# Moving the narrowing of weight pieces on VectorE's and ScalarE's queues in a fused attention, soft-MoE and MLP kernel

## The chip, the cores and the metric

The kernel runs on one core of a Trainium2 chip. The metric is the device time of one execution in microseconds (us); the median of three runs of the kernel before is 685.01 us (684.3 to 691.0).

## The reference

Attention over 4 batches of 12 heads, 448 tokens, 64 dimensions, with normalised q and k, gives a matrix `x` of 1792 tokens by 768. A soft mixture of 8 experts with 4 slots each follows, and then a two-layer MLP with a leaky activation:

```python
logits = x @ phi
d = softmax of logits over tokens;  c = softmax of logits over slots
slot_input = (d.T @ x).reshape(E, 4, 768)
h = np.maximum(slot_input[e] @ w1[e], 0.0)        # per expert e
slot_out[e] = h @ w2[e]
x = c @ slot_out
h = x @ w_in
g = np.maximum(h, 0.0) + alpha * np.minimum(h, 0.0)
out = g @ w_out
```

The inputs are float32, but `w_in` and `w_out` are float64 and reach the kernel as pairs of 32-bit words; "narrowing" a piece of them (128 rows by 768) means making float32 numbers of it with integer operations.

## The kernel before, in words

**Stages.** Attention runs up to about 308 us of the profile. The expert stage follows (315 to 417 us), then a short stage that multiplies the slots' outputs S into `w_in` (L1396 to L1447, to about 428 us), and then the main loop of the MLP (L1528 to L1530), which runs to the end.

**Order.** From attention on, the program's order is written out by hand (`manual_schedule`): each engine works through its own queue in the order in which the program issues instructions, and an instruction that waits holds up all behind it on that engine. All large transfers are issued by SP (SyncE), in program order too.

**The expert loop** (`for e in range(E)`). For each of 8 experts: PE multiplies the slots' inputs by the first layer, 24 matmuls of 512 columns (L1339); ScalarE copies the two halves to `h_sb` (L1350); PE transposes them (L1353); VectorE sums columns (L1355) and takes the maximum with 0 (L1361) into `hT`; PE multiplies by the second layer, 32 matmuls of 384 columns (L1370), which accumulate S in `pS`. The weights come in units of 1536 KB, four to an expert (two for each layer), through 11 buffers in rings; unit n waits until unit n - 11 has been read (`prefetch`, L475).

**Side work in that loop.** `turn_c(b)`, for experts 2 to 5, prepares the dispatch weights of batch b: two casts on VectorE (L1262), two subtractions on GpSimd (L1263), four transposes on PE (L1267), one copy on ScalarE to `cT4` (L1270). `turn_alpha` (expert 3) transposes `alpha` on PE (L1252) and copies it on VectorE (L1253, L1254). `narrow_in(n)` finishes the pieces 8 to 15 of `w_in`: one Abs on ScalarE (L540), then five operations on VectorE (L541, L543, L545, L548, L551), through two buffers `wf`.

**w_out.** `fetch_out(n)` (L1281) loads a raw piece pair into a ring buffer: the pairs 0 and 1 into the buffers of expert 5's second-layer weights, issued on SP ahead of the last six weight units, which are units 26 and 27 (expert 6, second layer) and 28 to 31 (expert 7); the pairs 2 and 3 after the loop; pair 4 inside `wide_out(1)`, pair 5 inside `wide_out(3)`. `wide_out(f)` is a generator of seven steps for piece f: Abs on ScalarE (L498), four operations on VectorE (L500, L502, L506, L510), then (for odd f the next fetch and) a cast to `whi` on ScalarE (L1301), then a subtraction to `wlo` on VectorE (L1303). `go_early` takes steps of it for pieces 0 to 3 in expert 6, ahead of that expert's L1370; `whi` and `wlo` of these pieces lie in the buffers of units 26 and 27. Pieces 4 to 15 are made in the main loop.

**After the loop** VectorE and ScalarE copy S to `s_sb` (L1396), PE folds it (L1402), and the `w_in` stage begins.

Of the kernel before, what the change touches and what calls it, by code (L numbers as in the profile page):

```python
# [353 lines left out]
def fused_attention_softmoe_mlp(  # L354
# [18 lines left out]
    E, _, FE = w1.shape  # L373
# [47 lines left out]
    def pst():  # L421
        return ps.tile([P, 512], F32, tag="t", name="pst", bufs=PST)
# [66 lines left out]
    def prefetch(n):  # L489
        while len(loaded) < min(n, len(items)):  # L490
            for _ in fetch():
                pass
# [43 lines left out]
    def narrow_in(n):  # L536
        g, i = divmod(n, 4)
        w = win[g][:, i * DM : (i + 1) * DM]
        t = hp.tile([P, DM], F32, tag="wf", name="wf", bufs=2)
        nc.scalar.activation(t, w, AF.Abs)  # L540
        nc.vector.tensor_scalar_max(t, t, F64_TINY)  # L541
        b = hp.tile([P, DM], U32, tag="wf", name="wb", bufs=2)
        nc.vector.tensor_copy(b, low[:, (n - N0) * DM : (n - N0 + 1) * DM])  # L543
        t, w = t.bitcast(U32), w.bitcast(U32)
        nc.vector.tensor_scalar(  # L545
            out=t, in0=t, scalar1=3, scalar2=0x3FFFFFFF, op0=ALU.logical_shift_left, op1=ALU.bitwise_and
        )
        nc.vector.scalar_tensor_tensor(  # L548
            out=t, in0=b, scalar=5, in1=t, op0=ALU.logical_shift_right, op1=ALU.bitwise_or
        )  # L550
        nc.vector.scalar_tensor_tensor(  # L551
            out=w, in0=w, scalar=0xC0000000, in1=t, op0=ALU.bitwise_and, op1=ALU.bitwise_or
        )
# [685 lines left out]
    def psa():  # L1239
        return ps.tile([P, 512], F32, tag="a", name="psa", bufs=6)  # L1240
# [8 lines left out]
    def turn_alpha():  # L1249
        pt = pst()  # L1250
        for t in range(2):
            nc.tensor.transpose(pt[:, t * 8 : t * 8 + 8], alpha_n[:, t::2], ident[: KF // 2, : KF // 2])  # L1252
        nc.vector.tensor_copy(alpha_t, pt[:, :KF].rearrange("p (t n) -> p n t", t=2))  # L1253
        nc.vector.tensor_scalar_mul(nalpha, alpha_t, -1.0)  # L1254
# [3 lines left out]
    def turn_c(b):  # L1258
        c = cN[:, b]
        cs = hp.tile([P, 4, 2, 2, NS], F32, tag="h_sb", name="cs")  # L1260
        for r in range(2):
            nc.vector.tensor_copy(cs[:, :, r, 0, :].bitcast(F32R), c)  # L1262
            nc.gpsimd.tensor_tensor(out=cs[:, :, r, 1, :], in0=c, in1=cs[:, :, r, 0, :], op=ALU.subtract)  # L1263
        pc = pst()
        for j in range(4):
            n = P if j < 3 else D
            nc.tensor.transpose(  # L1267
                pc[:, j * P : j * P + n], cs[:n, j].rearrange("p a b s -> p (a b s)"), ident[:n, :n]
            )
        nc.scalar.copy(  # L1270
            cT4[:, b * S : (b + 1) * S].rearrange("k (p c) -> k c p", c=NC),
            pc[:, :S].rearrange("k (c p) -> k c p", c=NC),
        )
# [5 lines left out]
    def fetch_out(n):  # L1279
        rawo[n] = raw = rings[1 - n % NW // (NW - NWI)][1].tile([P, UNIT], F32, tag="w", name="rawo").bitcast(U32)  # L1280
        nc.sync.dma_start(raw, w_out[2 * n * P : 2 * (n + 1) * P, :].bitcast(U32).rearrange("(p t) f -> p (t f)", p=P))  # L1281
# [10 lines left out]
    def wide_out(f):  # L1292
        src = rawo[f // 2].rearrange("p (n w) -> p n w", w=2)[:, (f % 2) * DM : (f % 2 + 1) * DM, :]
        if f % 4 == 0:
            w_pair(f // 4)
        hi, lo = w_tile(f)
        wf = wfs[0].tile([P, DM], F32, tag="wf", name="wf", bufs=wfs[1])
        yield from narrow(wf, src, nc.vector)
        if f % 2 == 1 and f // 2 + NW < KF // 2:
            fetch_out(f // 2 + NW)  # L1300
        nc.scalar.copy(hi, wf)  # L1301
        yield
        nc.vector.tensor_tensor(out=lo, in0=wf, in1=hi.bitcast(F32), op=ALU.subtract)  # L1303
        got.add(("wo", f))
# [5 lines left out]
    wfs = (hp, 2)  # L1310
    NEARLY = 4
    early = {f: wide_out(f) for f in range(NEARLY)}
    EARLY_STEPS = [0, 1, 0, 0, 0, 0, 0, 2, 1, 1, 1, 1, 0, 1, 3, 2, 2, 2, 2, 1, 2, 3, 3, 3, 3, 2, 3, 3]

    def go_early():
        for f in EARLY_STEPS:
            next(early[f], None)

    order = ExitStack()
    order.enter_context(tc.manual_schedule())  # L1320
    pS = [psa() for _ in range(2)]
    NARROW = ((8, 9), (10, 11), (12, 13), (14, 15), (), (), (), ())
    for e in range(E):
        n = min(NRING + 4 * e, len(items))
        if len(loaded) <= T["RAWPOS"] < n or (e == E - 1 and not rawo):
            prefetch(T["RAWPOS"])
            for i in range(NEARLY // 2):
                fetch_out(i)
        prefetch(n)
        if e == 1:  # L1330
            nc.sync.dma_start(alpha_n, alpha.rearrange("(n f) -> n f", n=KF // 2))
        ph = [psa() for _ in range(2)]
        seen = set()
        todo = [(0, 0, 0), (0, 1, 1), (0, 2, 2), (1, 0, 3), (1, 1, 0), (1, 2, 1)]
        todo += [(0, 3, 3), (0, 4, 0), (0, 5, 1), (1, 3, 2), (1, 4, 3), (1, 5, 0)]
        last = {(hf, g): t for hf, t, g in todo}
        for hf, t, g in todo:
            wu = loaded[0, e, t // 3].rearrange("p (t f) -> p t f", t=3)
            nc.tensor.matmul(  # L1339
                ph[hf][32 * g : 32 * g + 32, :],  # L1340
                slT[:, t, :],
                wu[:, t % 3, hf * 512 : (hf + 1) * 512],
                start=(hf, g) not in seen,
                stop=last[hf, g] == t,
                tile_position=(0, 32 * g),
            )
            seen.add((hf, g))
        for hf in range(2):
            h_sb = hp.tile([P, 512], F32, tag="h_sb", name="h_sb")
            nc.scalar.copy(h_sb, ph[hf])  # L1350
            pt = pst()
            for t in range(4):
                nc.tensor.transpose(pt[:, t * P : (t + 1) * P], h_sb[:, t::4], ident)  # L1353
            dst = hT[:, e, hf * 4 : hf * 4 + 4, SPE * e : SPE * e + SPE]
            nc.vector.tensor_reduce(  # L1355
                out=dst,
                in_=pt.rearrange("p (f g s) -> p f s g", f=4, g=4)[:, :, SPE * e : SPE * e + SPE, :],
                axis=AX.X,
                op=ALU.add,
            )  # L1360
            nc.vector.tensor_scalar_max(dst, dst, 0.0)  # L1361
        if e == E - 2:
            go_early()
        for n in NARROW[e]:
            narrow_in(n)
        for u in range(2):
            wu = loaded[1, e, u].rearrange("p (t f) -> p t f", t=4)
            for hf in range(2):
                for g in range(4):
                    nc.tensor.matmul(  # L1370
                        pS[hf][32 * g : 32 * g + 32, :HD],
                        hT[:, e, 4 * u + g, :],
                        wu[:, g, hf * HD : (hf + 1) * HD],
                        start=(e == 0 and u == 0),
                        stop=(e == E - 1 and u == 1),
                        tile_position=(0, 32 * g),
                    )

        if e == 3:
            turn_alpha()  # L1380
        if 2 <= e < 2 + B:
            turn_c(e - 2)

    while len(rings) > 3:
        rings.pop()[0].close()
# [247 lines left out]
```

## Time and profile before

| | |
|---|---|
| median of 3 runs | 685.01 us (684.3 to 691.0) |
| the profiled execution | 685.3 us, its span 683.3 us |
| PE matmul busy | 616.2 us, 90% of the span |
| VectorE (DVE) busy | 464.9 us, 68% |
| ScalarE (ACT) busy | 372.4 us, 54% |
| GpSimd (POOL) busy | 191.6 us, 28% |
| chain that ended last | PE 63%, ACT 14%, DMA 9%, DVE 8%, POOL 4% |

All times are microseconds from the start of the span, of one execution. PE is TensorE's matmuls, PEld its weight loads, SPq SyncE's queue of DMA issues. Busy shares are means over stages with different limits, so the rows are read by stage.

### The profile page before, as it was taken

The numbers are of one execution on the slowest core, as the hardware profiler recorded it, in microseconds if no ns is written. First come the engines' busy times: TensorE is split into PE (matmuls) and PEld (weight loads), VectorE is DVE, ScalarE is ACT, GpSimd is POOL, SyncE is SP. The second block draws the span as 40 slices with busy tenths as digits, with TensorE's granted clock in tenths as the row PEclk, the third lists the DMA queues.
The fourth block names the chain that finished last, engine by engine and source line by source line (L and its number), as shares of the span: only waits on it lengthen the run. The fifth ranks groups of instructions, "written<-read, shape, count | busy, mean of one in ns | idle before, by whom it ended". The sixth has DMA issues, their size and how long they took to land.

```text
span 683.3 us, 14166 instructions
## 1 busy us (share of the span) xinstructions
PE 616.2 (90%) x5670; PEld 475.9 (70%) x5670; DVE 464.9 (68%) x921; ACT 372.4 (54%) x717; POOL 191.6 (28%) x203
## 2 busy tenths in 40 slices
PE   0799998989999999998868668999999999999997
PEld 0367665666667777764323214888899999999997
DVE  5788999998789877735941444999964545454540
ACT  3799998889999998742321223776521111111110
POOL 6976666557657764111001000000000000000000
PEclk9999999999999999999988969999999999999999
DMA  4575677364456325499999799130020101010101
GB/s 138 133 239 165 188 211 204 110 189 126 131 143 200 99 76 171 123 350 391 425 424 395 283 423 400 67 120 0 1 93 1 47 1 47 1 47 0 47 1 46
DMA packets 36240, 106.89 MB, mean 156 GB/s; under 512 B 5448, under 2 KB 22352, under 8 KB 31824
## 3 DMA queue, kind: packets, MB, share of 16 engines
q1 hardware_dynamic: 36176, 106.01, 44.7%
q8 instruction: 44, 0.72, 0.5%
q14 instruction: 20, 0.16, 0.1%
HBM read 92.18 MB, written 5.51 MB: 143 GB/s over the span
## 4 chain that ended last, share of the span: by engine, by line
PE 63%; ACT 14%; DMA 9%; DVE 8%; POOL 4%; issue 2%; SPq 1%; ACTq 0%; POOLq 0%; DVEq 0%
PE psa L1530 12%; PE psa L1529 12%; PE psa L1528 11%; PE psn L818 5%; DMA unit<-in_moe_w_dram 4%; PE psv L878 4%; PE psv L868 3%; PE psa L1339 3%; ACT e L834 3%; PE psr L800 2%; DMA q<-q 2%; ACT psn L839 2%; POOL nf L717 2%; PE psa L1370 2%; ACT sp L723 1%
## 5 line engine op out<-in xcount | busy, mean ns | idle before, releaser
L1528 PE MATMUL psa<-whi,gh 128*128 128x384 f32 (+1 forms) x448 | 152.0, 339 | 0.0
L1529 PE MATMUL psa<-wlo,gh 128*128 128x384 f32 (+1 forms) x448 | 151.1, 337 | 0.0
L1530 PE MATMUL psa<-whi,gl 128*128 128x384 f32 (+1 forms) x448 | 150.8, 337 | 0.0
L809 DVE TENSOR_REDUCE m<-psr 128x1 f16<-128x448 f32 x168 | 97.7, 615 | 4.8 <-PE psr L800 4.6
L1497 ACT CAST gh<-t 128x512 fp32r<-128x512 f32 x40 | 24.9, 621 | 123.0 <-DVE t L1494 122.5
L1529 PEld LDWEIGHTS psa<-wlo,gh 128*128 128x128 f32 x448 | 84.2, 188 | 2.7
L1528 PEld LDWEIGHTS psa<-whi,gh 128*128 128x128 f32 x448 | 84.2, 188 | 2.7
L1530 PEld LDWEIGHTS psa<-whi,gl 128*128 128x128 f32 x448 | 84.1, 188 | 2.8
L878 PE MATMUL psv<-vH,e 128*128 128x65 f16 (+1 forms) x1152 | 84.2, 194 | 0.0
L878 PEld LDWEIGHTS <-e 128*128 128x128 f16 (+1 forms) x1728 | 79.3, 106 | 0.0
L1491 DVE TENSOR_SCALAR t<-pst,alpha_t 128x256 f32<-128x256 f32 x80 | 34.9, 476 | 62.9 <-PE pst L1485 62.9
L868 PEld LDWEIGHTS psv<-vR,e 128*128 128x128 f32 (+1 forms) x384 | 58.9, 176 | 20.0 <-issue 10.8
L878 PE MATMUL psv<-vL,e 128*128 128x64 f16 (+1 forms) x576 | 72.5, 193 | 0.0
L850 POOL TENSOR_TENSOR e<-ef,e 128x448 f16<-128x448 f32 x48 | 52.0, 1083 | 72.2 <-ACT ef L839 52.7
L868 PE MATMUL psv<-vR,e 128*128 128x65 f32 (+1 forms) x384 | 69.8, 263 | 0.2 <-PE psn L818 0.2
L834 ACT ACTIVATE e<-psn 128x448 f16<-128x448 f32 x120 | 65.2, 544 | 7.5 <-PE psn L818 6.2
L818 PE MATMUL psn<-q,k 128*128 128x448 f16 (+1 forms) x192 | 61.4, 361 | 7.3 <-DMA q<-q 2.0
L818 PE MATMUL psn<-qB,kB 67*128 67x448 f16 (+1 forms) x192 | 61.0, 357 | 1.6 <-DMA qB<-mr 1.4
L800 PE MATMUL psr<-k,q 128*128 128x448 f16 (+1 forms) x192 | 57.2, 374 | 3.5 <-ACT k L752 2.8
L850 DVE TENSOR_TENSOR e<-psn,e 128x448 f16<-128x448 f32 x72 | 44.4, 617 | 21.4 <-ACT psn L839 21.2
L730 POOL TENSOR_TENSOR sp<-nf,sp 128x448 f16<-128x448 f32 x48 | 49.8, 1047 | 12.2 <-ACT sp L723 11.8
L745 PE MATMUL pst<-ident,sp 128*128 128x128 f16 x336 | 27.7, 230 | 17.4 <-POOL sp L730 17.4
(178 smaller groups left out, 1091.2 us busy)
## 6 DMA issues: line engine op xcount, KB each, us to landing
unit<-in_moe_w_dram SPq DMA_DIRECT2D x26, 1536.0 KB, 12.2
unit<-in_moe_w_in_dram SPq DMA_DIRECT2D x24, 512.0 KB, 6.8
rawo<-in_moe_w_out_dram SPq DMA_DIRECT2D x8, 1536.0 KB, 13.2
unit<-in_moe_w_dram SPq DMA_DIRECT2D x36, 256.0 KB, 4.9
qk<-in_q_dram SPq DMA_DIRECT2D x12, 448.0 KB, 3.8
qk<-in_k_dram SPq DMA_DIRECT2D x12, 448.0 KB, 5.4
out_dram<-osb SPq DMA_DIRECT2D x14, 384.0 KB, 2.3
vR<-in_v_dram SPq DMA_DIRECT2D x24, 128.0 KB, 3.8
```

Of the source, the lines that this page charges most:

```text
L730: eng.tensor_tensor(out=d["sp"][:, a, :, D:], in0=d["nf"][:, a], in1=d["sp"][:, a, :, 0:D], op=ALU.subtract)
L800: nc.tensor.matmul(pn[o0:o1, :S], d["q"][:, c0 : c0 + o1 - o0], d["k"][:, h * S : (h + 1) * S], start=True, stop=True)
L809: nc.vector.tensor_reduce(out=d["m"][:, c : c + 1], in_=d.pop(("pn", c))[:, :S], axis=AX.X, op=ALU.max)
L818: nc.tensor.matmul(pe[o0:o1, :S], lhs[:, c0 : c0 + o1 - o0], rhs[:, h * S : (h + 1) * S], start=st_, stop=not st_,)
L834: nc.scalar.activation(e2[:, 0], pe[:, :S], AF.Exp, scale=0.125)
L850: eng.tensor_tensor(out=e2[:, 1], in0=ef, in1=e2[:, 0], op=ALU.subtract)
L868: nc.tensor.matmul(pv[o0:o1, slot, :], d["e", c][:, qs], d["vv"][:, h, sl * D : 4 * D + 1], start=(j == 0), stop=False,)
L878: nc.tensor.matmul(pv[o0:o1, slot, 0:wd], d["e", c][:, w // 2, qs], (vl if w == 1 else vh)[:, 4 * h + sl, 0:wd], start=(j == 0 and w == 0) ...
L1491: nc.vector.tensor_scalar(out=t0[:, cs], in0=ph[:, cs], scalar1=0.0, scalar2=alpha_t[:, f // 2, i : i + 1], op0=ALU.min, op1=ALU.mult)
L1528: nc.tensor.matmul(a, gh[f][:, ms], hi[:, hs], start=(f == 0 and not (packed and m % 2 == 1 and hf == 0)), stop=False)
L1529: nc.tensor.matmul(a, gh[f][:, ms], lo[:, hs], start=False, stop=False)
L1530: nc.tensor.matmul(a, gl[f][:, ms], hi[:, hs], start=False, stop=(f == KF - 1 and not (packed and m % 2 == 0 and hf == 1)))
```

## The change

In `narrow_in`'s schedule the pieces of an expert are taken at the end of its loop body, after L1370, `turn_alpha` and `turn_c`, instead of ahead of L1370; and piece 15 moves from expert 3 to expert 4. Since VectorE and ScalarE don't take part in L1370, the places on their queues differ only for experts 2 to 4, where `turn_c` and `turn_alpha` now come first. `go_early` is cut in two: in expert 6 all steps of the pieces 0 and 1 and the first five of piece 2; in expert 7, behind its column sums, the last two steps of piece 2 and all seven of piece 3.

```diff
-    EARLY_STEPS = [0, 1, 0, 0, 0, 0, 0, 2, 1, 1, 1, 1, 0, 1, 3, 2, 2, 2, 2, 1, 2, 3, 3, 3, 3, 2, 3, 3]
-
-    def go_early():
-        for f in EARLY_STEPS:
+    EARLY_STEPS = (
+        (0, 1, 0, 0, 0, 0, 1, 1, 1, 1, 0, 0, 2, 1, 1, 2, 2, 2, 2),
+        (2, 3, 2, 3, 3, 3, 3, 3, 3),
+    )
+
+    def go_early(part):
+        for f in EARLY_STEPS[part]:
             next(early[f], None)
...
-    NARROW = ((8, 9), (10, 11), (12, 13), (14, 15), (), (), (), ())
+    NARROW = ((8, 9), (10, 11), (12, 13), (14,), (15,), (), (), ())
     for e in range(E):
...
             nc.vector.tensor_scalar_max(dst, dst, 0.0)
-        if e == E - 2:
-            go_early()
-        for n in NARROW[e]:
-            narrow_in(n)
+        if e >= E - 2:
+            go_early(e - E + 2)
         for u in range(2):
...
             turn_alpha()
         if 2 <= e < 2 + B:
             turn_c(e - 2)
+        for n in NARROW[e]:
+            narrow_in(n)
```

## Rows read from the trace of the kernel before

**Rows 1.** Windows: each engine's busy time, granted clock, DMA share, GB/s.

```profile
345.00:362.00 17.00, 11.23 (x70) 4.14 (x70) 7.96 (x18) 3.73 (x5) 0.86 (x2) 0.80 1.01 424
...
426.00:500.00 74.00, 72.99 (x418) 62.93 (x411) 68.87 (x103) 47.60 (x79) 0.00 (x0) 1.00 0.12 45
```

**Rows 2.** Windows of 2 us around the pause of the DMA queue, same columns.

```profile
374.00:376.00 2.00, 2.00 (x22) 0.59 (x15) 0.00 (x0) 0.58 (x1) 0.00 (x0) 1.00 0.33 131
376.00:378.00 2.00, 1.95 (x10) 0.83 (x7) 0.18 (x1) 1.17 (x2) 0.00 (x0) 1.00 0.00 0
...
380.00:382.00 2.00, 2.00 (x26) 0.79 (x20) 0.00 (x0) 0.00 (x0) 0.21 (x1) 1.00 0.51 92
```

**Rows 3.** Waits of SP's queue, 300 to 430: us in total, times, longest.

```profile
SPq L1281 <- PE psa L1370: 15.4, 2, 14.5
```

**Rows 4.** Chain that ended last, in order of time: start, us, what.

```profile
384.40 27.12 DMA unit<-in_moe_w_dram
411.52 0.57 ACT h_sb L1350
```

**Rows 5.** Timeline of experts 2 and 3: start, us; in brackets idle time before.

```profile
344.29 1.20 PE L1267 MATMUL pst<-ident,cs 128*128 128x128 f32 x4 [5.77 <-POOL cs L1263]
...
345.42 6.03 PE L1339 MATMUL psa<-unit,slT 128*32 128x512 f32 x24
...
360.09 0.17 DVE L1253 COPY alpha_t<-pst 128x16 f32<-128x16 f32 x1
...
361.69 1.20 PE L1267 MATMUL pst<-ident,cs 128*128 128x128 f32 x4 [5.72 <-POOL cs L1263]
```

**Rows 6.** Timeline of expert 5, without side work ahead of it.

```profile
372.81 0.75 PE L1267 MATMUL pst<-ident,cs 128*128 128x128 f32 x4
...
373.49 3.62 PE L1339 MATMUL psa<-unit,slT 128*32 128x512 f32 x24
373.59 0.99 ACT L1270 CAST cT<-pst 128x448 fp32r<-128x448 f32 x1 [4.24 <-PE pst L1267]
...
378.51 2.79 PE L1370 MATMUL psa<-unit,hT 128*32 128x384 f32 x32
...
378.88 0.17 DVE L1361 TENSOR_SCALAR hT<-hT 128x16 f32<-128x16 f32 x1
...
380.07 1.62 SPq L1281 DMA_DIRECT2D rawo<-in_moe_w_out_dram  x2
```

**Rows 7.** Timeline of one narrowed piece of w_in and its successor, expert 3.

```profile
353.31 0.55 DVE L541 TENSOR_SCALAR wf<-wf 128x768 f32<-128x768 f32 x1
...
355.82 0.84 ACT L540 ACTIVATE wf<-win 128x768 f32<-128x768 f32 x1 [2.96 <-DVE wf L548]
...
356.70 0.56 DVE L541 TENSOR_SCALAR wf<-wf 128x768 f32<-128x768 f32 x1
```

**Rows 8.** Timeline of PE where experts 6 and 7 wait for weights.

```profile
394.07 2.79 PE L1370 MATMUL psa<-unit,hT 128*32 128x384 f32 x16 [7.06 <-DMA unit<-in_moe_w_dram]
...
397.77 2.79 PE L1370 MATMUL psa<-unit,hT 128*32 128x384 f32 x16 [0.91 <-DMA unit<-in_moe_w_dram]
...
401.38 3.63 PE L1339 MATMUL psa<-unit,slT 128*32 128x512 f32 x12 [0.82 <-DMA unit<-in_moe_w_dram]
...
405.98 1.91 PE L1339 MATMUL psa<-unit,slT 128*32 128x512 f32 x12 [0.97 <-DMA unit<-in_moe_w_dram]
```

**Rows 9.** Timeline from w_out's piece 3 to the S copy and piece 4.

```profile
407.59 0.56 DVE L500 TENSOR_SCALAR wf<-wf 128x768 f32<-128x768 f32 x1 [0.99 <-ACT wf L498]
...
410.65 1.94 DVE L1303 TENSOR_TENSOR wlo<-wf,whi 128x768 fp32r<-128x768 f32 x2
410.76 0.83 ACT L1301 CAST whi<-wf 128x768 fp32r<-128x768 f32 x1 [2.48 <-DVE wf L510]
...
416.79 0.56 DVE L1396 COPY s_sb<-psa 128x384 f32<-128x384 f32 x1 [2.20 <-PE psa L1370]
...
428.29 0.92 ACT L498 ACTIVATE wf<-rawo 128x768 f32<-128x768 f32 x1
```

## The prediction

> **What bounds the kernel now.** I read the windows by stage first, then the chain of waits, then the timeline of the experts. From 426 us on PE is busy 72.99 of 74 us at 2.4 GHz, and that loop runs so to the end [rows 1]; an edit ahead of it is worth what it moves the loop's start. Ahead of it, in the expert stage, the bound is another: from 345 to 362 us the DMA engines are full (share 1.01, 424 GB/s) while PE is busy 11.23 of 17 us [rows 1]. A unit of 1536 KB is 1.573 MB and so takes 3.7 us; four make an expert, 14.8 us, while PE needs about 8.4 us for one (expert 5 below). The weights set the pace, as long as their queue never runs dry.
>
> It runs dry once. The DMA share is 0.33 in 374 to 376 us, 0.00 in the next two slices and 0.51 in 380 to 382 [rows 2]: idle 1.3 + 2 + 2 + 1.0 = 6.3 us. The waits tell why: SP's line 1281, the fetch of w_out's raw pieces, waits 14.5 us for PE's L1370 [rows 3]. It needs the buffers of expert 5's second-layer weights, and the last six weight units stand behind it in SP's queue. The chain goes from that issue to the last unit's issue at 384.40, over its landing, to ScalarE's copy at 411.52 [rows 4].
>
> So PE's progress to expert 5 matters only because it releases SP. What holds PE back is seen at expert 2 [rows 5]: the transposes of the dispatch weights (L1267) wait 5.77 us for GpSimd's subtraction, which waits for VectorE's casts, which stand behind two narrowed pieces on VectorE. PE then comes back at 1.2 GHz: L1339 takes 6.03 us against 3.62 in expert 5 [rows 5, 6]. Expert 3 repeats both (two such places in all).
>
> **The change, part by part.** No instruction is added or removed; only places in the queues of VectorE and ScalarE change. For experts 0 and 1 nothing stands between the old and the new place but PE's own work, so their queues stay as they are: nothing gained, nothing lost.
>
> A piece costs 0.84 us on ScalarE and 3.39 us on VectorE (353.31 to 356.70); the next Abs starts when the first OR is done, about 1 us ahead of the piece's end [rows 7].
>
> *Experts 2 to 4, walked through.* Expert 2's L1370 ends at 344.29 - 5.77 = 338.52. The casts and GpSimd's subtraction (within 1.6 us, 360.09 to 361.69 in expert 3 [rows 5]) now run during it, so the transposes (0.75 us) end at 339.3 and L1339 of expert 3 (3.62) at 342.9 [rows 5, 6]. ScalarE's order is now the cT copy (0.99, to 340.3), then Abs. VectorE narrows piece 12 from 341.1 to 344.5, piece 13 to 347.9. What is late next: expert 3's h_sb copies stand behind the second Abs (to 344.4), and its column sums behind piece 13, so L1370 runs 348.3 to 351.1. Then alpha's transposes on PE, and behind them, exposed, VectorE's alpha copies, casts and GpSimd, 2.0 us together (0.4, and 360.09 to 361.69) [rows 5], transposes and L1339 to 357.4; piece 14 holds VectorE from 355.6 to 359.0; L1370 359.4 to 362.2. Expert 4 the same with piece 15 (364.8 to 368.2): expert 5's L1370 starts at 368.6. SP issues 1.56 us after that start (378.51 to 380.07) [rows 6], so at 370.2, 9.9 us earlier than now.
>
> How early is early enough? The queue is empty at about 374.7, and an issue at 380.07 moved bytes from about 381.0 [rows 2, 6], so 373.8 suffices. The margin is 3.6 us. The units for expert 5 are there in time: the last of the stream ends at 374.7, so the third before it, the first that L1370 of expert 5 needs, ends at about 364. The whole idle time goes: **6.3 us** earlier for each of the last six units. PE can't use the other 3.6 us, since the DMA stream is then full throughout.
>
> One price can eat the margin. PE is busy only about 1.5 us from 342.9 to 348.3. If the clock falls there, expert 3's L1370 takes twice as long: 16 matmuls in 2.79 us at 1.2 GHz [rows 8] against 32 in 2.79 [rows 6], 2.8 us more. Below is nothing, above 2.8 plus 2.4 for a slow L1339 [rows 5, 6]. One stretch of it fits in the margin; I take nothing.
>
> *The tail.* Units 26 to 29 are met by PE's waits at 394.07, 397.77, 401.38 and 405.98 [rows 8]; the last two follow at 3.7, about 409.7 and 413.4. In the new order: 387.8, 391.5, 395.1, 399.7, 403.4 and 407.1. Pieces 0 and 1 keep their waits (the buffers of expert 6's units, read by 391.5 + 2.79 = 394.3); two subtractions, a cast and piece 2's 3.1 us of VectorE end about 401, before the last column sums can come. SP issues the fetch of w_out's raw pair 4 about 387.5, behind the six units, and it delays none of them.
>
> Now, with go_early whole in expert 6, the last expert's h_sb copy starts at 411.52 [rows 4] although its matmuls ended at 407.89 (405.98 + 1.91) [rows 8]. Yet the last unit comes only at 413.4, so L1370 could have ended at about 414.8; it let the S copy start at 416.79 [rows 9]. The old place thus cost **2.0 us**. In the new order the second half of L1339 starts at 399.7 and takes 1.91 us at 2.4 GHz or 3.63 at 1.2 GHz (the two halves of expert 7 before) [rows 8]. From its end to the second column sum expert 5 needs 1.95 us (377.11 to 379.05) [rows 6]: 403.6 or 405.3. Then VectorE still has piece 2's subtraction (0.97), piece 3's four operations (407.59 to 410.73, 3.14), a wait of 0.83 for its cast and its subtraction (0.97) [rows 9], 5.9 us, all ahead of the S copy: 409.5 or 411.2. L1370 itself ends at 407.1 + 1.4 (half of expert 5's 2.79) = 408.5 and hides most of this; **0.9 to 2.7 us** stay exposed. Against 416.79 the S copy comes 7.3 or 5.6 us earlier. Either clock is possible: before, PE came back to work at 394.07 and had 2.4 GHz again only for the second half. I take the slow one: the row nearest to it is the restart behind the 7.06 us wait for unit 26 [rows 8], which the new order has too, about 8 us long (379.8 to 387.8).
>
> SP's fetch of pair 5 now comes after piece 3's last OR (407.6 to 409.3), and pairs 2 and 3 queue behind it. With pair 4 ending at 410.8 and pair 5 at 414.5, pair 2 lands at 418.2. ScalarE's Abs on it stands at 428.29, 11.5 us after the S copy [rows 9]: now 421.0 or later. Slack 2.8 us; no cost.
>
> **The clock after the tail.** PE pauses before and after the last unit's 1.4 us, then waits for VectorE. At expert 2 an idle time of 5.77 us was followed by 1.2 GHz [rows 5]; the new pauses are shorter, about 2.3 and 1.5 to 3.3 us, with work between. If the clock is low there, the S stage, nearly all PE, pays for it. Bounds: nothing, or half of 3.6 us of work (as long as the slow L1339 half [rows 8]), 1.8 us. I take nothing if the L1339 half was slow, since PE was then busy without a break up to 406 us; with a fast one the two prices come out alike.
>
> The Trainium skill, "TensorE: Matmul & The Clock Gate", section "HAM oscillation — how this bites in real kernels", says that waits inside a matmul loop put the array back to half rate again and again, and each restart is paid. Rows 5 agree for 5.77 us. By that rule both prices would be due and the sum would be 3.8 us; by the rows alone, one.
>
> **Sum.** 6.3 (queue never dry) + 2.0 (old place) - 2.7 (piece 3 ahead of the S copy) = 5.6 us. The profiled execution took 685.3 us (span 683.3), 0.3 above the median of 685.01: 685.3 - 5.6 = **679.7 us**.
>
> **Rivals.**
> - *The clock costs nothing*: 2.4 GHz for the last L1339 half and the S stage. 685.3 - 7.4 = 677.9. For it: the same half ran fast before. Against it: that needs the clock back by 399.7. Chance 0.26.
> - *Both clock prices*: 685.3 - 3.8 = 681.5. Against it: shorter pauses than any the rows show to be followed by a fall. Chance 0.14. The page named above speaks for it.
> - *The queue still runs dry*: PE's gap in expert 3 drops the clock for longer than one L1370, and SP issues after 373.8. With a slow L1370 and a slow L1339, 370.2 + 5.2 = 375.4, 1.6 us of gap stay: 681.3; if nothing is gained on the queue, the S copy comes at 407.9 + 1.95 + 5.9 = 415.8 instead of 416.79: 684.3. Chance 0.09.
> - *Slower*: the same place, once it goes on: if the clock stays at 1.2 GHz from expert 3 through expert 5, three L1370 (2.8 each), two L1339 (3.6 each) and transposes (1) add 16.6, less 1.5 that VectorE hides: SP issues at 385.3, 5.2 us later than before, and with the tail's 1.0 the end is 4.2 us later: 689.5. It decides from an issue after 381.1. Against it: from 345 to 362 us, with two idle times of this kind, the granted clock was 0.80 in the mean, so it came back in between [rows 1]. Chance 0.05.
> - The forecast, one of the two prices paid, 678.4 to 681.0: chance 0.46.
>
> **Range and chances.** Within 1% is about what a measurement of this kernel can't tell from no change; 1% is 6.9 us, so faster by over 1% is below 678.2. That takes the first rival and little else: 0.28. Slower by over 1% is above 691.9, where the slow rival reaches only in part: 0.04. Within 1%: 0.68. The range takes the first three cases and the forecast, from 677.0 (a tail better by 0.9) to 682.6.
>
> **What would show it.** Right: DMA share at 1.0 through 370 to 410 with no slice near 0; SP's L1281 at 370 to 373; L1267 of experts 2 and 3 within 2 us of L1370; VectorE's last L1303 just before the S copy (L1396) at 409 to 412; the last loop unchanged. Wrong: an idle slice still there; PE at 1.2 GHz from 348 to 370; a wait of ScalarE's L498 for rawo ahead of the loop; an S copy that waits for PE and not for VectorE.

## The result

The median after is 681.35 us (678.84 to 684.24, 4 runs), beside 688.0 us (684.3 to 693.76, 4 runs) before: ratio 0.9893 [0.9852, 0.9934], 1.07% less. Two further sets of the same pair gave 0.9903 [0.987, 0.9937] and 0.9903 [0.9872, 0.9933], about 6.7 us (the medians of the three sets differ by 6.7, 6.5 and 8.3 us). The profiled execution took 680.03 us with a span of 678.2; the prediction was 679.7 us in the range 677.0 to 682.6. Two terms of its sum were off, in opposite directions, by 1 to 2 us each. How that was found takes up most of what follows.

Line numbers after: L1339 of before is L1342, L1353 is L1356, L1361 is L1364, L1370 is L1371, L1396 is L1399, L1402 is L1405, L1528 is L1531; L1267, L1281, L1301, L1303 and those of the narrowing keep theirs.

The windows of the kernel after, for the stretches of [rows 1, 2] (columns as there):

```profile
345.00:362.00 17.00, 11.19 (x70) 4.10 (x69) 8.76 (x20) 3.42 (x5) 0.87 (x2) 0.80 1.01 425
374.00:376.00 2.00, 2.00 (x29) 0.78 (x24) 0.26 (x2) 0.00 (x0) 0.88 (x2) 1.00 0.98 412
376.00:378.00 2.00, 2.00 (x21) 0.72 (x15) 0.00 (x0) 0.78 (x1) 0.00 (x0) 1.00 1.02 430
...
380.00:382.00 2.00, 1.98 (x13) 0.53 (x14) 0.00 (x0) 0.59 (x1) 0.00 (x0) 1.00 0.98 412
372.00:410.00 38.00, 24.03 (x159) 8.13 (x162) 18.41 (x35) 9.40 (x14) 0.88 (x2) 0.78 1.01 424
426.00:500.00 74.00, 74.00 (x418) 64.93 (x417) 68.44 (x104) 45.02 (x75) 0.00 (x0) 1.00 0.16 57
```

The pause is gone: the DMA share is 0.98 to 1.02 in the slices that had 0.33, 0.00 and 0.51, and 1.01 over 372 to 410. The main loop is PE's as before, and it lasts 251.3 us from its first L1531 to the last copy of its results in both kernels.

The timeline of PE and of SP's queue in experts 2 to 5 after answers to [rows 5, 6]:

```profile
338.78 2.79 PE L1371 MATMUL psa<-unit,hT 128*32 128x384 f32 x32
341.49 0.75 PE L1267 MATMUL pst<-ident,cs 128*128 128x128 f32 x4
342.17 3.62 PE L1342 MATMUL psa<-unit,slT 128*32 128x512 f32 x24
347.84 1.24 PE L1356 MATMUL pst<-ident,h_sb 128*128 128x128 f32 x8 [2.04 <-ACT h_sb L1353]
351.23 4.19 PE L1371 MATMUL psa<-unit,hT 128*32 128x384 f32 x32 [2.15 <-DVE hT L1364]
...
357.36 1.08 PE L1267 MATMUL pst<-ident,cs 128*128 128x128 f32 x4 [1.61 <-POOL cs L1263]
358.37 4.88 PE L1342 MATMUL psa<-unit,slT 128*32 128x512 f32 x24
...
364.67 2.79 PE L1371 MATMUL psa<-unit,hT 128*32 128x384 f32 x32
...
373.71 2.79 PE L1371 MATMUL psa<-unit,hT 128*32 128x384 f32 x32 [0.55 <-DVE hT L1364]
...
375.27 1.62 SPq L1281 DMA_DIRECT2D rawo<-in_moe_w_out_dram  x2
```

The transposes of the dispatch weights (L1267) follow expert 2's second layer without a wait and expert 3's after 1.61 us; they waited 5.77 and 5.72 us before. Instead expert 3's L1371 and expert 4's L1342 run partly at 1.2 GHz: 4.19 and 4.88 us, where 2.79 and 3.62 stand at 2.4 GHz.

The timeline of PE where it waits for the last units, for [rows 8]:

```profile
391.21 2.79 PE L1371 MATMUL psa<-unit,hT 128*32 128x384 f32 x16 [7.79 <-DMA unit<-in_moe_w_dram]
394.90 2.79 PE L1371 MATMUL psa<-unit,hT 128*32 128x384 f32 x16 [0.90 <-DMA unit<-in_moe_w_dram]
398.52 5.61 PE L1342 MATMUL psa<-unit,slT 128*32 128x512 f32 x24 [0.83 <-DMA unit<-in_moe_w_dram]
...
406.00 1.50 PE L1371 MATMUL psa<-unit,hT 128*32 128x384 f32 x16 [0.44 <-DMA unit<-in_moe_w_dram]
409.71 1.50 PE L1371 MATMUL psa<-unit,hT 128*32 128x384 f32 x16 [2.21 <-DMA unit<-in_moe_w_dram]
```

And the chain that ended last, from the last weight issue on it to the `w_in` stage, for [rows 4, 9]:

```profile
378.36 23.82 DMA unit<-in_moe_w_dram
...
402.22 1.91 PE psa L1342 x12
...
405.86 0.18 DVE hT L1364
406.03 0.86 DVE wlo L1303
406.89 0.48 DVE wf L500
...
408.98 0.97 DVE wf L510
...
409.97 0.84 ACT whi L1301
...
410.84 0.04 DVE wlo L1303
410.87 0.84 issue
411.71 0.56 DVE s_sb L1399
```

Unit 29 comes at 402.22, and from the last column sum (405.86) VectorE's work on pieces 2 and 3 leads to the S copy at 411.71. The last unit's matmuls, 409.71 to 411.21, are half a microsecond ahead of it: weights and VectorE end almost together.

### The profile page after: what moved, and what is told of

Read it like the earlier page. It is cut to its first block, busy times and chain, and to the rows that moved or that the text cites. A ratio compares the mean times of both kernels' runs of the same rounds, so it can differ in the third digit from the quotient of the medians.

```text
span 678.2 us, 14166 instructions
## 1 busy us (share of the span) xinstructions
PE 617.0 (91%) x5670; PEld 477.9 (70%) x5670; DVE 464.6 (68%) x921; ACT 372.3 (55%) x717; POOL 192.0 (28%) x203
## 4 chain that ended last, share of the span: by engine, by line
PE 63%; ACT 15%; DVE 8%; DMA 6%; POOL 4%; issue 3%; SPq 0%; ACTq 0%; POOLq 0%; DVEq 0%
PE psa L1532 12%; PE psa L1533 12%; PE psa L1531 12%; PE psn L818 5%; DMA unit<-in_moe_w_dram 4%; PE psv L878 4%; PE psv L868 3%; ACT e L834 3%; PE psa L1371 2%; PE psa L1342 2%; PE psr L800 2%; ACT psn L839 2%; POOL nf L717 2%; ACT sp L723 2%; ACT e L832 1%
## 5 line engine op out<-in xcount | busy, mean ns | idle before, releaser
L1531 PE MATMUL psa<-whi,gh 128*128 128x384 f32 (+1 forms) x448 | 152.0, 339 | 0.0
L1531 PEld LDWEIGHTS psa<-whi,gh 128*128 128x128 f32 x448 | 84.2, 188 | 2.7
L850 DVE TENSOR_TENSOR e<-psn,e 128x448 f16<-128x448 f32 x72 | 44.4, 617 | 21.7 <-ACT psn L839 19.3
```

Of the source, the lines that this page charges most:

```text
L850: eng.tensor_tensor(out=e2[:, 1], in0=ef, in1=e2[:, 0], op=ALU.subtract)
L1531: nc.tensor.matmul(a, gh[f][:, ms], hi[:, hs], start=(f == 0 and not (packed and m % 2 == 1 and hf == 0)), stop=False)
```

## Whether the two profiles can be compared as they stand

Attention is the same code in both kernels, yet expert 0 begins at 315.42 us in the profile before and at 318.46 in the profile after; the places where TensorE's granted clock was low lay elsewhere (among others at 108 and at 313 us after, at neither before). Measured from expert 0, the change looked worth 8.1 us: the S copy came 101.4 us behind it before (416.79) and 93.3 after. Counted from the start of the span it was worth 5.1. Four more profiles settle which is nearer. Two are of the kernel after:

> The changed kernel once more, beside the others on one chip. Theory: the stretch from expert 0 to the S copy is 93.3 us as in its first profile, within 1 us; the time falls by 5 to 8 us; what differs from the first profile lies ahead of expert 0, where attention took 318.5 us instead of 315.4 and nothing was changed. Rival (the change itself makes attention longer): attention takes 318 us again.

> The changed kernel again, as the measure for the three runs beside it on one chip. Theory: S copy at 411.6 us within 1 us of the span, whatever attention took, since the DMA stream and not PE's start sets it; ratio to before 0.988 to 0.993. Rival (the S copy follows expert 0's start): it moves with the end of attention, which was at 318.5 and 316.2 us in the two profiles so far.

and, later, two of the kernel before:

> The kernel before once more, one profile, to see what its S copy follows. Theory: in it SP's fetch of the raw pieces waits for PE at expert 5, so everything behind hangs on the end of attention, one to one: with e0 the start of the first L1339 of expert 0, SP's L1281 is at e0 + 64.7 (within 1.5; clock falls in the experts account for that), the S copy at e0 + 101.4 (within 1.5), the main loop 251.3 long. Rival: the S copy comes at 416.8 (within 1) whatever e0 is, since the weights' stream, which starts long before e0, sets it; then the 3.0 us that attention was longer in the changed kernel's profile were not lost, and the change is worth 5.1, not 8.1. The DMA pause (a slice of 2 us at 0.00 near 378) is there by both.

> The same as the run ahead of it, for a second value of e0, the start of expert 0: theory SP's L1281 at e0 + 64.7 and the S copy at e0 + 101.4, each within 1.5; rival: the S copy at 416.8 within 1 whatever e0 is.

All in us from the start of the span; the idle time of the DMA queue is worked out from windows of 4 us, (1 - share) x 4 where the share is under 0.97. The first of its columns also takes in the end of attention (shares of 0.75 to 0.92 from 300 to 308 in some profiles) and leaves out what lies ahead of 300, so it is good to about 1 us.

| | expert 0 | queue idle 300 to 330 | idle 370 to 390 | SP L1281 | unit 26 met | S copy | loop starts | span |
|---|---|---|---|---|---|---|---|---|
| before | 315.42 | 1.1 | 6.4 | 380.07 | 394.07 | 416.79 | 428.80 | 683.3 |
| before, again | 320.47 | 2.9 | 4.2 | 384.63 | 398.71 | 420.38 | 432.40 | 686.9 |
| before, third | 319.86 | 3.0 | 4.2 | 384.03 | 397.87 | 419.57 | 431.58 | 686.1 |
| mean | 318.6 | 2.3 | 4.9 | 382.9 | 396.9 | 418.9 | 430.9 | 685.4 |
| after | 318.46 | 2.2 | 0 | 375.27 | 391.21 | 411.71 | 423.67 | 678.2 |
| after, again | 316.23 | 3.6 | 0 | 374.77 | 391.01 | 411.57 | 423.53 | 678.1 |
| after, third | 321.57 | 3.1 | 0 | 380.30 | 395.56 | 416.37 | 428.53 | 683.1 |
| mean | 318.8 | 3.0 | 0 | 376.8 | 392.6 | 413.2 | 425.2 | 679.8 |

Expert 0 begins at the same mean time in both, so the means may be compared: 5.7 us at the S copy and at the loop, 5.6 in the span. Neither theory of the four expectations held in full. In the kernel before SP's issue follows expert 0 one to one (64.2 to 64.7 us behind it), and the S copy nearly does (99.7 to 101.4). It comes 1.5 to 1.7 us closer to expert 0 in the two later profiles: 0.5 of that lies ahead of SP's issue and 1.0 behind unit 26, where PE read unit 27 in 1.50 us (16 matmuls of L1370) instead of 2.79, so that `go_early` had its buffers sooner. In the kernel after the S copy stood at 411.6 to 411.7 for two starts 2.2 us apart and came 4.7 us later with the third. There SP begins its unbroken run of weight issues at 289.26, 286.46 and 292.85: the start of the stream moves with attention too, and unit 26 is met 102.0, 104.6 and 102.7 us behind it, latest in the profile with the longest pause of the queue.

That pause is one of two. The windows of the second profile of the kernel before:

```profile
320.00:324.00 4.00, 3.55 (x20) 0.91 (x22) 0.36 (x1) 0.00 (x0) 1.81 (x1) 0.57 0.66 276
324.00:328.00 4.00, 4.00 (x32) 1.84 (x30) 1.34 (x6) 1.91 (x3) 0.00 (x0) 1.00 0.73 255
...
380.00:384.00 4.00, 3.95 (x28) 1.76 (x26) 1.06 (x6) 1.17 (x2) 0.11 (x1) 1.00 0.34 141
384.00:388.00 4.00, 4.00 (x44) 1.53 (x39) 0.00 (x0) 0.98 (x1) 0.78 (x2) 1.00 0.61 184
```

I had seen only the second. The first belongs to expert 0: from 296 to 332 us SP's longest wait is for PE's first layer, to free buffers. The waits of SP's queue in that stretch (us in total, times, longest), of the profile I predicted from:

```profile
SPq L475 <- PE psa L1339: 16.7, 4, 13.3
```

and the same of the kernel after, in its second profile, which has the longest first pause:

```profile
SPq L475 <- PE psa L1342: 19.5, 4, 16.0
```

What the queue loses in the first pause it no longer loses in the second. Both together were 7.4, 7.1 and 7.3 us before and 2.2, 3.6 and 3.1 after: means 7.3 and 3.0, so 4.3 us less idle time; unit 26 comes 4.3 us earlier (396.9 to 392.6). The profile I predicted from had the shortest first pause of the six, and so the longest second one.

Unit 26 is not the best place to count, though. The traces hold sixteen landings for each unit, as many as there are DMA engines, and PE's wait ends with the last. In the first profile before, those of unit 28 come from 400.42 to 401.34 and those of unit 29 from 404.12 to 405.94: the first are 3.7 us apart, the last 4.6, because one of the sixteen parts fell 0.9 us behind, and the spread stays so up to unit 31 (411.52 to 413.34). The two other profiles before have the same step at the same unit (spread 0.95 to 1.80 and 0.67 to 1.51 us). In the kernel after the spread is 2.0 to 2.5 us already at unit 26. In the kernel before it is 1.7 to 1.9 us ahead of the pause and 0.7 to 1.0 for the first transfer behind it: the pause brings the sixteen parts together again. In the kernel after, without that pause, they stay apart. What made the one part late is not shown: a 16 KB transfer of instructions, 1.1 us long, falls between units 28 and 29 in all six profiles, but moves the last landing in the three before alone. Counted at the last landing of unit 31, the end of the stream, the weights come 97.2 to 97.9 us behind expert 0 before and 91.1 to 93.2 after, and the S copy 2.5 to 3.5 and 2.1 to 2.4 us later: of the 5.7 us, 5.1 are the queue's and 0.6 the tail's.

The same landings correct the reading of [rows 4]. At 411.52 the first part of unit 31 landed, which ScalarE's copy to `h_sb` does not read; that copy stood behind the cast of piece 3 on ScalarE's queue. The chain of the second profile before leads to it from unit 27, over the work on the pieces:

```profile
386.88 15.40 DMA unit<-in_moe_w_dram
...
402.41 1.53 PE psa L1370 x16
...
414.83 0.59 ACT h_sb L1350
```

## The parts, one at a time

**The narrowing alone.** The pieces move as in the change; `go_early` stays whole in expert 6.

```diff
-    NARROW = ((8, 9), (10, 11), (12, 13), (14, 15), (), (), (), ())
+    NARROW = ((8, 9), (10, 11), (12, 13), (14,), (15,), (), (), ())
...
-        for n in NARROW[e]:
-            narrow_in(n)
         for u in range(2):
...
             turn_c(e - 2)
+        for n in NARROW[e]:
+            narrow_in(n)
```

> Only w_in's pieces are moved behind turn_c; go_early stays whole in expert 6. Theory (the queue of DMAs runs dry once because SP waits for expert 5): no slice of DMA share near 0 from 370 to 410 us, the stretch from expert 0's first L1339 to the S copy falls from 101.4 us to about 95.1, and the time by about 6.3 us. Rival (most of the gain is go_early's split): the stretch falls by 2 us at most. Rival (PE's idle time at experts 2 and 3, 5.8 us and a slow L1339 each, is itself on the path): it falls by 10 us or more.

Measured: 683.8 us beside 688.36, ratio 0.9942 [0.9913, 0.9971], 4.0 us. The queue is full in the stretch of the pause (share 1.00 over 372 to 390), as expected, but less is gained: the S copy comes 97.1 us behind expert 0, where the theory had 95.1. The timeline of its tail:

```profile
392.25 2.79 PE L1368 MATMUL psa<-unit,hT 128*32 128x384 f32 x16 [7.77 <-DMA unit<-in_moe_w_dram]
...
408.93 0.83 ACT L1301 CAST whi<-wf 128x768 fp32r<-128x768 f32 x1 [2.49 <-DVE wf L510]
409.67 1.07 ACT L1350 COPY h_sb<-psa 128x512 f32<-128x512 f32 x2
411.80 4.06 PE L1368 MATMUL psa<-unit,hT 128*32 128x384 f32 x32
415.29 0.56 DVE L1396 COPY s_sb<-psa 128x384 f32<-128x384 f32 x1 [2.95 <-PE psa L1368]
```

Behind the cast of piece 3 the last expert's h_sb copy waits until 409.67, so all 32 matmuls of the last layer come after 411.80, and the S copy comes 23.0 us behind unit 26, where the three profiles before have 21.7 to 22.7, and 4.0 us behind the last landing of unit 31 (411.32). The weights come earlier; the tail takes part of it back.

**`go_early` alone.** The kernel after, with the narrowing where it was.

```diff
         if e >= E - 2:
             go_early(e - E + 2)
+        for n in NARROW[e]:
+            narrow_in(n)
...
-        for n in NARROW[e]:
-            narrow_in(n)
```

with `NARROW` as before.

> Only go_early is split; w_in's pieces stay where they were. Theory: the pause of the DMA queue stays at about 6.3 us, the last unit comes as late as before, and the S copy gains only the 1.0 us by which piece 3's end (415.8) is ahead of 416.8: the stretch from expert 0 to the S copy falls from 101.4 to about 100.4, the time by 1.0. Rival (the split is the larger part): 4 us or more, since the last h_sb copy comes 3.6 us earlier.

Measured: 689.21 us, ratio 1.002 [0.9979, 1.006]. Its windows still have the pause:

```profile
376.00:380.00 4.00, 3.95 (x29) 1.42 (x22) 0.16 (x1) 1.77 (x3) 0.00 (x0) 1.00 0.73 302
380.00:384.00 4.00, 4.00 (x44) 1.86 (x48) 0.91 (x6) 0.00 (x0) 0.88 (x2) 1.00 0.23 49
```

The last unit's matmuls begin at 415.64 and the S copy comes 2.0 us later (417.63), as in the kernel after, 98.2 us behind expert 0. Behind the last landing it is 2.1 us, where the profiles before have 2.5 to 3.5, so the cut of `go_early` is worth 0.3 to 1.3 us here. The stage behind the S copy gave more than that back, at a granted clock of 0.80 instead of 1.00; it took 14.2 us up to the loop, and 12.0 in the kernel before:

```profile
417.63:431.80 14.17, 12.56 (x119) 7.39 (x118) 5.18 (x12) 5.93 (x14) 0.00 (x0) 0.80 0.78 328
```

PE comes to it out of waits of 2.21 and 0.60 us. How often the clock falls there one profile can't tell; in the ten runs nothing is left of the gain. The cut gives more once the weights come earlier: from 4.0 us behind the last landing (narrowing alone) to 2.1 to 2.4 (the whole change). So the parts, 4.0 and nothing measurable, don't add up to the 6.7 us of both. By the times alone that is not certain, since the three have intervals of 2.0, 2.8 and 2.3 us to either side; the traces give it a reason.

**SP's queue, with PE left as it was.** Is it PE's idle time that costs, or that SP's fetch of the raw pieces holds the units back? In the kernel before, the fetch goes behind units 26 and 27 instead of ahead of them.

```diff
-    "RAWPOS": 26,
+    "RAWPOS": 28,
```

> The queues of VectorE and ScalarE stay as before; the two raw fetches of w_out are issued behind units 26 and 27 instead of ahead of them. Theory (only SP's wait counts): SP still waits for expert 5 until about 380, but two units (7.4 us) keep the DMA engines busy over it; no idle slice, the last unit lands about 6.3 us earlier, and as go_early's pieces start about 1 us later than before the S copy gains some 5.8 us: stretch about 95.6. Rival (PE's idle time at experts 2 and 3 is what costs): no gain, stretch 101 to 102, since that idle time is untouched.

Measured: 684.95 us, ratio 0.996 [0.9934, 0.9986], 2.8 us faster. The timeline of PE and of ScalarE, and the window of the pause:

```profile
348.76 1.20 PE L1267 MATMUL pst<-ident,cs 128*128 128x128 f32 x4 [5.76 <-POOL cs L1263]
...
365.17 1.20 PE L1267 MATMUL pst<-ident,cs 128*128 128x128 f32 x4 [5.72 <-POOL cs L1263]
...
392.25 1.70 ACT L498 ACTIVATE wf<-rawo 128x768 f32<-128x768 f32 x2 [3.07 <-DMA rawo<-in_moe_w_out_dram]
...
376.00:378.00 2.00, 2.00 (x20) 0.78 (x21) 0.00 (x0) 0.99 (x1) 0.00 (x0) 1.00 1.01 420
```

PE idles at experts 2 and 3 as before, and the queue never runs dry (no slice of 2 us under 0.92 from 324 to 416). The last unit has landed 92.5 us behind expert 0 (410.72), as early as in the kernel after, and 97.2 to 97.9 before. So PE's idle time delays the weights only through the fetch that stands ahead of the units on SP. I had expected 5.8 us; the raw pieces now land later, `go_early` ends later, the last h_sb copy waits until 410.08, and the S copy stands at 415.60, 97.4 us behind expert 0 where I had 95.6. The rival's 101 to 102 fell.

**Both remedies.** The same shift in the kernel after:

> The changed kernel with the raw fetches two units later in SP's queue (RAWPOS 28 for 26), so SP's wait on expert 5 can't empty the queue even if PE is late. Theory: the DMA queue is full from 324 to 410 us in the changed kernel as it is, so nothing is gained: last unit at the same place, S copy at 411.7 (within 1) or 93 to 95 after expert 0 starts, time within 0.3% of the changed kernel's ratio to before (0.990). Rival A: PE's pace still decides (raw fetches wait for expert 5's second layer); then S copy 1 to 3 us earlier, time ratio 0.986 to 0.988. Rival B: the raw pieces come 7.4 us later, VectorE narrows them later, piece 3 ends later and the S copy comes 1 to 4 us later, as it did where the kernel before had the raw fetches there; ratio 0.992 to 0.996.

Measured: 682.88 us, ratio 0.9907 [0.9864, 0.995], the same as the kernel after; its first Abs waits 8.47 us for raw pieces (392.59), and the S copy comes at 413.97, 94.9 behind expert 0. A queue that is already full gains nothing from units issued earlier. The stage behind the S copy took 13.4 us here, at a granted clock of 0.87. The interval leaves room for 1 to 2 us lost in the tail, so the theory and rival B are not told apart by the time.

**The tail.** Is it worth more to get piece 3 off the S copy's way? Its last two steps go behind the copy, and S is put into another buffer, so that the copy waits for no pool to open.

```diff
-        (2, 3, 2, 3, 3, 3, 3, 3, 3),
+        (2, 3, 2, 3, 3, 3, 3),
+        (3, 3),
...
+    s_sb = low.bitcast(F32)[:, :DM]
+    copies = (nc.vector.tensor_copy, nc.scalar.copy)
+    for hf in range(2):
+        copies[hf](s_sb[:, hf * HD : (hf + 1) * HD], pS[hf][:, :HD])
+    go_early(2)
...
-    s_sb = hc.tile([P, DM], F32, tag="osb", name="s_sb")
-    copies = (nc.vector.tensor_copy, nc.scalar.copy)
-    for hf in range(2):
-        copies[hf](s_sb[:, hf * HD : (hf + 1) * HD], pS[hf][:, :HD])
```

> The changed kernel with the last two steps of w_out's piece 3 (cast and subtraction) behind the S copies; S goes to another buffer for that. Theory (piece 3 ahead of the S copy is the exposed remainder of the tail): VectorE's S copy no longer waits for the last L1303 and follows PE's L1371, about 0.6 to 1.2 us earlier against the last unit's matmuls; the time falls by that much against the changed kernel, hardly more than can be measured. Rival (the S stage waits for something else): the S copy is earlier and the main loop's start is not.

Measured: 682.71 us, ratio 0.9946 [0.9919, 0.9974]: no gain over the kernel after. The S copy did come 0.9 us behind the start of the last unit's matmuls (L1372 here) instead of 2.0, but the stage behind it gave that back:

```profile
409.14 1.50 PE L1372 MATMUL psa<-unit,hT 128*32 128x384 f32 x16 [2.21 <-DMA unit<-in_moe_w_dram]
...
410.05 0.56 DVE L1391 COPY low<-psa 128x384 f32<-128x384 f32 x1 [0.68 <-PE psa L1372]
...
411.94 0.96 DVE L1303 TENSOR_TENSOR wlo<-wf,whi 128x768 fp32r<-128x768 f32 x1 [1.33 <-ACT whi L1301]
...
413.10 0.26 DVE L1408 COPY ST<-pst 128x96 f32<-128x96 f32 x1 [0.20 <-DVE wlo L1303]
413.50 1.93 PE L1419 MATMUL psa<-win,ST 128*32 128x256 f32 x32 [1.31 <-DVE ST L1408]
```

The copy of the folded S (L1408) now stands behind the postponed subtraction (L1303), and PE waits 1.31 us for it. From the S copy to the loop it takes 12.98 us instead of 11.96.

**The weights still earlier.** Two kernels fetch raw pair 1 behind the last unit, so the units stand one transfer (3.7 us) earlier in the queue. In the first, pieces 2 and 3 are left to the main loop (their steps in `EARLY_STEPS` go as well):

```diff
-    NEARLY = 4
+    NEARLY = 2
...
-            for i in range(NEARLY // 2):
-                fetch_out(i)
+            fetch_out(0)
         prefetch(n)
+        if e == E - 2:
+            fetch_out(1)
```

> The changed kernel with w_out's raw pair 1 fetched behind the last weight unit, and its pieces 2 and 3 made in the main loop like the pieces 4 to 15. Theory (the stage is now bound by the DMA stream alone): the last unit lands 3.7 us earlier and the S copy comes 3 to 4 us earlier, but VectorE, busy 68.9 of 74 us in the first part of the main loop, gets 9.8 us more to do there, so PE waits in the loop and the time stays within 2 us of the changed kernel's. Rival (the stage is bound by PE): the S copy does not move.

in the second the steps of piece 2 and the first two of piece 3 are mixed into the `w_in` stage by hand, and the other five of piece 3 into the beginning of the main loop:

> As the run before it, but the steps of the pieces 2 and 3 stand among the S stage's work and not behind it. Theory: the S copy again 3 to 4 us earlier than in the changed kernel, most of the 9.8 us of VectorE fit beside the S stage's 12 us, in which VectorE has little to do, and the time is 2 to 3.5 us below the changed kernel's. Rival (VectorE's and ScalarE's order in the S stage gives it back): the stretch from the S copy to the main loop grows from 12.0 to 15 us or more and nothing is gained.

Measured: 684.02 us, ratio 0.9941 [0.9912, 0.9971], and 680.97 us, ratio 0.9911 [0.988, 0.9943]. The S copy comes at 409.36 and 407.92, 91.1 and 88.6 us behind expert 0, but the main loop grows from 251.3 to 255.6 and 254.6 us. In the second kernel PE waits for VectorE where it waited for nothing in the kernel after; the window 440 to 500, first of the kernel with mixed steps and then of the kernel after:

```profile
440.00:500.00 60.00, 58.94 (x323) 49.38 (x323) 55.56 (x85) 35.17 (x59) 0.00 (x0) 1.00 0.14 53
```

```profile
440.00:500.00 60.00, 60.00 (x340) 52.71 (x339) 54.56 (x84) 35.18 (x59) 0.00 (x0) 1.00 0.12 45
```

PE's busy time differs by 1.1 us, but its matmuls by 17 (323 beside 340), which is 3.0 us at the 0.18 us that one takes in the second window (60.00 over 340): nearly all of the 3.3 falls here, where VectorE is busy 55.56 of 60 us. The first kernel pays at the clock as well: from 410 to 416 its granted clock is 0.52 in the mean, and from the S copy to the loop it takes 16.5 us, 2.60 of them a wait of PE for ScalarE. No version measured is better than the kernel after by more than its interval.

## Why the prediction held, step by step

- *The bound.* Right. The weights' stream sets the S copy, the main loop follows unchanged, and the pause of the queue came from SP's line 1281. The experiment with SP's queue (`RAWPOS` 28 in the kernel before) shows it without touching PE.
- *The walk through experts 2 to 5.* The profile after starts expert 0 3.0 us later. With that added, expert 3's L1370 was forecast at 351.3 and came at 351.23. Then the price that I took as nothing was due: 1.4 us on L1371, 0.3 on the transposes and 1.3 on L1342, within the bounds of nothing to 5.2. SP issued at 375.27, 2.1 us behind the walk's 373.2. The step "One stretch of it fits in the margin; I take nothing" was right in its first half alone: 3.0 us were due, and they did fit. Unit 26 is met 14.0 us behind the issue when the queue is empty (before) and 15.9, 16.2 and 15.3 us behind it after; by that estimate 1.3 to 2.2 of the margin of 3.6 us were left. The Trainium skill, "TensorE: Matmul & The Clock Gate", section "HAM oscillation — how this bites in real kernels", has waits inside a matmul loop put the array back to half rate; the 4.19 and 4.88 us, behind waits of 2.04, 2.15 and 1.61, agree.
- *6.3 us for the queue.* In the first pair of profiles, from expert 0 on, 5.9: unit 26 was due at 390.8 with the shift and came at 391.21, and units 27 to 31 within 0.5. Over three profiles each it is 4.3 at unit 26 and 5.1 at the last landing of unit 31. The step "It runs dry once" failed: it runs dry twice, and the two pauses share what there is. I took the second pause of one execution for its size in all.
- *2.0 us for the old place of `go_early`, less 2.7 for piece 3.* Forecast -0.7 together; measured from unit 26 to the S copy, +1.4 over three profiles (22.0 to 20.6) and +2.2 in the first pair; from the last landing of unit 31, +0.6 and +1.3. Three pieces of the sum account for nearly all of the difference of 2.9 in the first pair. The slow half of L1339 (1.7) was not paid: the half behind unit 29 took 1.91 us after. Unit 29 came 3.7 us behind unit 28, where I had copied the 4.6 us of the profile before (0.9). The remaining 0.2 is VectorE: from the column sum to the S copy 5.7 us, forecast 5.9. The 4.6 us were no spacing of the stream but the one late part of unit 29, and so belong to the weights and not to the tail.
- *The rule and the rows.* By the rule both clock prices would have been due in the tail, 681.5 us; after the wait of 7.79 us PE did restart at 1.2 GHz (16 matmuls in 2.79 us), but the rate was back at 401.9, in time for unit 29, and the `w_in` stage took 11.96 us after and 12.01 before. Neither price in the tail was paid: as to the clock, the rival "the clock costs nothing" was nearer than the forecast, which had the slow half of L1339 as a term. That does not refute the rule: in the third profile after the half behind unit 29 took 2.17 us and the `w_in` stage 12.16, at a granted clock of 0.96, and with `go_early` alone the stage took 14.2 (0.80). The price exists, above the bound of 1.8 us that I had given it, and falls due in some executions.
- *The rivals.* "The queue still runs dry" fell (no slice near 0 from 330 to 410), and "slower" fell: PE's clock came back within experts 3 and 4 (L1371 of expert 4 takes 2.79 us). With 5.6 us in the sum and 5.6 measured over three profiles each, the size came out because the queue term was too large (by 2.0 us at unit 26, by 1.2 at the last landing) and the tail term too small by as much (2.1 and 1.3). That is luck, and so is the 680.03 of the profiled execution beside 679.7: its attention took 3.0 us longer than that of the profile before, and from expert 0 on it gained 8.1. Means of three profiles leave about 1 us open in each term.
- *Pair 2.* The first Abs after the S copy begins at 423.16 with no wait for a transfer: no cost, as forecast.
- *The chances.* I gave 0.68 to a change within 1%. The ratios, 1.07%, 0.97% and 0.97% less, stand on that bound, and their intervals reach to both sides. Three runs with a median of 685.01 were also a low estimate of the kernel before; the sets measured later have medians of 687.3 to 688.4.

## What to carry to other kernels

When a transfer queue runs dry, look for the instruction at its head and for what that one waits; PE's idle time delayed the weights here only because a fetch stood on it with six ready transfers behind. Count every pause of the queue in the stage and not just the longest, and take its size from more than one execution: pauses upstream and downstream trade against each other. Count a stream at its last transfer, since a transfer is there only when the slowest of its parts is. A part that is nearly hidden by a late transfer gains little alone, and gives it when the transfer comes earlier.

## What the runs showed that I had not expected

Attention, the same instructions in each kernel, ended between 315.4 and 321.6 us (start of expert 0), with the granted clock low in other stretches each time; that is as much as the whole change is worth, and it goes into the times of single executions. And the clock fell after shorter waits than the 5.77 us of [rows 5]: expert 3's second layer, granted 1.2 GHz in part, came behind two waits of PE of 2.04 and 2.15 us with 1.24 us of transposes between them.
